# A 128-row lead-in with in-place LayerNorm, and crossbar DMA transposes for blocks 1 to 3, in a fused attention and GEGLU kernel

## The chip, the cores and the metric

The kernel runs on one core of a Trainium2 chip. Its time is device microseconds of one execution; the median of several executions is compared. The engines are TensorE (PE for matmuls, PEld for its weight loads), VectorE (DVE), ScalarE (ACT), GpSimd (POOL) and SyncE (SP), which issues every DMA of this kernel. Each engine runs its own instruction list in order and waits on semaphores.

## The reference

The input x is 2048 rows of 512. It is normalized, and the result xn goes through two branches whose outputs are added to x.

```python
xn = (x - mean(x)) / sqrt(var(x) + 1e-5)              # per row
# branch A: 32 heads of 16, sliding window of 8 positions, 2 apart
q, k, v = split(xn @ wqkv)                             # wqkv [512, 1536]
logits[s, w] = q[s] . k[s - 2*w] / 4                   # masked where s - 2*w < 0
o[s] = sum_w softmax(logits)[s, w] * v[s - 2*w]
A = o @ wo                                             # [512, 512]
# branch B
B = (gelu_tanh(xn @ w_gate) * (xn @ w_up)) @ w_down    # 512 -> 1376 -> 512
out = x + A + B
```

All inputs, weights and the output are bf16.

## The kernel before, in words

**Blocks and stages.** The rows are worked in 4 blocks of 512 (`b`), each of two pairs `p` of 128-row tiles `t`. One block goes through these stages, with the names of their tiles:

1. LayerNorm: x comes from memory into XIN, two tiles at a time (L906 for pair 0, L910 for the others). DVE makes the statistics `st` (L921) and their aggregate `mv` (L925); POOL adds epsilon, `ve` (L930 for block 0, L948 for the others), and raises it to the power 0.5, `sq` (L936, L954); DVE takes the reciprocal, `rstd` (L942, L960). DVE subtracts the mean from XIN into a second buffer XN (L968) and scales it there (L975). XIN and XN have 2 slots of two tiles each.
2. Transpose: TensorE transposes the 128x128 pieces of XN through an identity into PSUM (L991), and ACT evicts them to `xnT` (L1002), which has the model dimension on the partitions. In block 0 that is done tile by tile (4 transposes), in the other blocks by pairs (8).
3. Projections: TensorE multiplies `Wqkv` with `xnT` (L1046) in groups of four matmuls, one for each 128 rows of the contraction. ACT evicts to QT (L1069), KT (L1076) and VT (L1083); VT goes to a scratch in memory (L1090). Block 0 is cut into two halves of 256 rows (`NHALF` is [2, 1, 1, 1]), so its matmuls are 256 columns wide; in the others they have 512.
4. Attention: DVE multiplies QT with shifted views of KT, eight products PROD of 128x2048 (L1105); TensorE sums them over the head dimension (L1120) into logits; softmax runs on DVE and ACT (L1153 to L1183), and the probabilities go through memory to the layout PT (L1191, L1198). Shifted bands BS of V come from memory (L1209), DVE multiplies them with PT (L1224, "PV products"), TensorE sums (L1243), and ACT evicts to OT (L1254).
5. Feed-forward: for each of 11 hidden tiles `j` (the last has 96 rows) two groups of four matmuls, with Wg and Wu (L1274); ACT applies GELU into GG (L1284) and evicts UU (L1291), and DVE multiplies them into HT (L1296).
6. Output: for each 128-row tile one PSUM sum of 11 matmuls with Wd (L1321) and four with Wo (L1334). DVE adds the row XR of x, loaded again (L1306), into OB (L1364), which is stored (L1371). The last two tiles are done in two halves.

Before the first transpose TensorE runs 9 warm-up matmuls on zeros (L855), two more behind the first transposes and four behind the second; all of them come before the first projection.

**What sets the order.** The program is a graph of tasks. Each task names its engine, an estimated duration, the items it reads and writes, and a priority. Buffers are slots of pools, and PSUM is a pool of 8 banks with a quota for each use. At build time a planner (`schedule`) places the tasks one by one on a modelled clock, by priority among those that can start early enough, and the result is a fixed instruction list for each engine. `order_after` adds an order between two tasks that share no data. The planner is run several times, and the pass with the shortest modelled time is taken. A DMA in the model takes a fixed time and a transfer time, and the transfers follow one another. So each edit to tasks, pools or priorities can change the order of everything behind it.

The lines that choose a block's order of work:

```python
base = b * PB_ + (p % 2) * 10 - 30 - (LN_SHIFT if b > 0 else 0)   # LayerNorm, LN_SHIFT = 960
base = b * PB_ - CHAIN_SHIFT[b]                                   # projections, attention, output
fb = FFN_BASE + b * FFN_STEP                                      # feed-forward: 500 + 1000 b
sched = dict(PE_SLACK=1.6, DMA_BPUS=250e3, ...)
```

A lower number goes first, so LayerNorm of a block is placed nearly a block ahead of its projections, and feed-forward of a block fills TensorE beside the attention of the same and the next block.

Of the kernel before, what the change touches and what calls it, by code (L numbers as in the profile page):

```python
# [141 lines left out]
class Graph:  # L142
# [118 lines left out]
    def schedule(self, params=None, prior=None):  # L261
# [86 lines left out]
        while nsched < ntot:  # L348
# [6 lines left out]
            for t in ready:  # L355
# [305 lines left out]
def bass_parallel_sum__sliding_local_dilated__glu_gated_geglu__prompt_kernel(nc, A_x, A_wqkv, A_wo, B_x, B_w_gate, B_w_up, B_w_down, out, dbg=None, cfg=None):  # L661
    cfg = dict(cfg or {})
    NXIN = cfg.get("NXIN", 2)
    NXN = cfg.get("NXN", 2)
    NQT = cfg.get("NQT", 2)
    NXT = cfg.get("NXT", 3)
    NPROD = cfg.get("NPROD", 4)
    NMS = cfg.get("NMS", 2)
    ACC_SPLIT = cfg.get("ACC_SPLIT", False)
    FIN_PE_FROM = cfg.get("FIN_PE_FROM", 99)  # L670
    FIN_PE = cfg.get("FIN_PE", False)
# [13 lines left out]
                                    acc=(4 if ACC_SPLIT else 2)))  # L685
# [5 lines left out]
    NHALF = cfg.get("NHALF", [2, 1, 1, 1])  # L691
    PVR_MERGE = cfg.get("PVR_MERGE", 2)
    R_ACCD = cfg.get("R_ACCD", 400)
# [11 lines left out]
    with contextlib.ExitStack() as es:  # L705
# [19 lines left out]
        mhalf = sb("mhalf", [128, 2], F32)  # L725
# [4 lines left out]
        mv = sb("mv", [128, NT, 2], BF)  # L730
        ve = sb("ve", [128, NT], F32)
        sq = sb("sq", [128, NT], BF)
# [3 lines left out]
        XN = sb("XN", [128, NXN, 2, 512], BF)  # L736
# [26 lines left out]
        P_xn = Pool("xn", NXN)  # L763
# [29 lines left out]
        I_mhalf = Item("mhalf")  # L793
# [4 lines left out]
        I_mv = Item("mv")  # L798
        I_ve = Item("ve")
        I_rstd = Item("rstd")  # L800
# [48 lines left out]
        WARM = cfg.get("WARM", (9, 2, 4))  # L849
# [10 lines left out]

        for i, nm in enumerate(("q", "k", "v")):
# [4 lines left out]
            G.task("sp", "ld_w" + nm, 0, mk(), wr=[(I_wq, nm)], prio=-900 + i, nbytes=512 * 1024)  # L866
# [3 lines left out]
        for ci, nj in enumerate(WCH):  # L870
# [4 lines left out]
            for (nm, Wx, I_w, src) in (("g", Wg, I_wg, B_w_gate), ("u", Wu, I_wu, B_w_up)):  # L875
                def mk(Wx=Wx, src=src, c_lo=c_lo, c_hi=c_hi):
                    return lambda e: e.dma_start(
                        Wx[:, :, c_lo:c_hi], src[:, c_lo:c_hi].rearrange("(k p) n -> p k n", p=128))
                G.task("sp", "ld_w%s%d" % (nm, ci), 0, mk(), wr=[(I_w, ci)], prio=R_WG + 2 * ci + (nm == "u"),
                       nbytes=(c_hi - c_lo) * 1024)  # L880
            j0 += nj
        G.task("sp", "ld_wd0", 0, lambda e: e.dma_start(
            Wd[:, 0:10, :], B_w_down[0:1280, :].rearrange("(j p) n -> p j n", p=128)),
            wr=[(I_wd, 0)], prio=R_WD, nbytes=1280 * 1024)
        G.task("sp", "ld_wd1", 0, lambda e: e.dma_start(
            Wd[0:96, 10, :], B_w_down[1280:1376, :]), wr=[(I_wd, 1)], prio=R_WD + 1, nbytes=96 * 1024)
        for d4 in range(4):
# [4 lines left out]
            G.task("sp", "ld_wo%d" % d4, 0, mk(), wr=[(I_wo, d4)], prio=R_WD + 2 + d4, nbytes=128 * 1024)  # L892
# [4 lines left out]
        for p in range(NP):  # L897
# [10 lines left out]
            else:  # L908
# [3 lines left out]
                G.task("sp", "ld_x%d" % p, 0, mk_ld(), wr=[(it_x, 0), (it_x, 1)], prio=-950 + p * 20,  # L912
# [4 lines left out]
            for t2 in range(2):  # L917
# [4 lines left out]
                G.task("dve", "bnst%d" % t, d_dve(512, 1.2), mk_st(), rd=[(it_x, t2)], wr=[(I_st, t)], prio=tp0(t))  # L922
# [3 lines left out]
                G.task("dve", "bnag%d" % t, 0.15, mk_ag(), rd=[(I_st, t)], wr=[(I_mv, t)], prio=tp0(t) + 1)  # L926
            if b == 0:
                for t in (2 * p, 2 * p + 1):
                    def mk_ve(t=t):
                        return lambda e: e.tensor_scalar(  # L930
                            out=ve[:, t:t + 1], in0=mv[:, t, 1:2], scalar1=1e-5, scalar2=1.0,
                            op0=ALU.add, op1=ALU.mult)
                    G.task("pool", "ve%d" % t, 0.19, mk_ve(), rd=[(I_mv, t)], wr=[(I_ve, t)], prio=tp0(t) + 2)

                    def mk_sq(t=t):
                        return lambda e: e.tensor_tensor(  # L936
                            out=sq[:, t:t + 1], in0=ve[:, t:t + 1], in1=mhalf[:, 0:1], op=ALU.pow)
                    G.task("pool", "sq%d" % t, 0.7, mk_sq(), rd=[(I_ve, t), I_mhalf], wr=[(I_sq, t)],
                           prio=tp0(t) + 3)

                    def mk_rs(t=t):
                        return lambda e: e.reciprocal(out=rstd[:, t:t + 1], in_=sq[:, t:t + 1])  # L942
                    G.task("dve", "rstd%d" % t, 0.15, mk_rs(), rd=[(I_sq, t)], wr=[(I_rstd, t)], prio=tp0(t) + 3)
            else:
                tt = (2 * p, 2 * p + 1)

                def mk_ve(p=p):
                    return lambda e: e.tensor_scalar(  # L948
                        out=ve[:, 2 * p:2 * p + 2], in0=mv[:, 2 * p:2 * p + 2, 1], scalar1=1e-5, scalar2=1.0,
                        op0=ALU.add, op1=ALU.mult)  # L950
                G.task("pool", "ve%d" % p, 0.19, mk_ve(), rd=[(I_mv, t) for t in tt], wr=[(I_ve, p)], prio=base + 2)

                def mk_sq(p=p):
                    return lambda e: e.tensor_tensor(  # L954
                        out=sq[:, 2 * p:2 * p + 2], in0=ve[:, 2 * p:2 * p + 2], in1=mhalf[:, :], op=ALU.pow)
                G.task("pool", "sq%d" % p, 0.75, mk_sq(), rd=[(I_ve, p), I_mhalf], wr=[(I_sq, t) for t in tt],
                       prio=base + 3)

                def mk_rs(p=p):
                    return lambda e: e.reciprocal(out=rstd[:, 2 * p:2 * p + 2], in_=sq[:, 2 * p:2 * p + 2])  # L960
# [480 lines left out]
```

## Time and profile before

| | |
|---|---|
| median of 3 executions | 207.98 us (207.72 to 208.19) |
| profiled execution | 207.99 us |
| span from its first to its last instruction | 206.2 us |
| granted TensorE clock | 1.000 |
| TensorE matmuls busy | 197.7 us, 96% of the span |
| DVE busy | 148.7 us, 72% |
| ACT busy | 109.9 us, 53% |
| POOL busy | 13.5 us, 7% |

Busy time is the union of an engine's instructions. An instruction row has its start, its duration, the engine, the line, the operation and the tiles; several like ones are merged (x8), and their duration is then that of the stretch. In brackets stands how long the engine was idle before, and what it waited for. Matmuls overlap: a 512-column matmul has a duration of 379 ns, but one starts about every 0.216 us. The chain of work goes back from the last instruction to what released each step. PEld is the weight load, which may run beside the matmul before it.

### The profile page before, as it was taken

Reading aid. Unit: us, or ns where it says so; the run is one execution under the profiler, and the core shown is the slowest. Engines: PE = TensorE matmul, PEld = TensorE weight load, DVE = VectorE, ACT = ScalarE, POOL = GpSimd, SP = SyncE. Lnnn points to the kernel's source line nnn. Section 1 sums busy time; section 2 is a strip of 40 time slices with the busy share of each in tenths; the row PEclk is TensorE's granted clock in tenths of the full one; section 3 lists DMA queues with packets and bytes.
Section 4 is the critical chain, followed back from the end, with each engine's and each line's share of the span. In section 5 each row is a group of like instructions: output and inputs, shape, how many; then the busy total and the mean of one; then the engine's idle time right before and its main releaser. Section 6 shows DMA issues by size and latency. Waiting matters only on the chain.

```text
span 206.2 us, 3162 instructions
## 1 busy us (share of the span) xinstructions
PE 197.7 (96%) x1197; PEld 93.4 (45%) x1197; DVE 148.7 (72%) x221; ACT 109.9 (53%) x188; POOL 13.5 (7%) x42
## 2 busy tenths in 40 slices
PE   7799999999899999999999999999999999997993
PEld 2487353444434445444443444433444443443483
DVE  3728799988999958968999949799775846122121
ACT  2476556996772007679849005784995005765000
POOL 6610011022000110000000000000000000000000
PEclk9999999999999999999999999999999999999999
DMA  5999936843548331044870173567021522000121
GB/s 163 378 400 356 225 93 166 212 96 114 137 131 205 97 102 54 7 107 132 206 163 0 55 201 104 133 146 184 0 51 52 156 78 76 0 3 0 40 74 38
DMA packets 27070, 25.45 MB, mean 123 GB/s; under 512 B 2896, under 2 KB 25520, under 8 KB 27056
## 3 DMA queue, kind: packets, MB, share of 16 engines
q1 hardware_dynamic: 27056, 25.26, 44.6%
q8 instruction: 9, 0.15, 0.3%
q14 instruction: 5, 0.04, 0.1%
HBM read 19.99 MB, written 5.26 MB: 122 GB/s over the span
## 4 chain that ended last, share of the span: by engine, by line
PE 66%; DVE 21%; DMA 5%; issue 3%; POOL 2%; ACT 1%; SPq 0%; DVEq 0%
PE PS L1274 22%; PE PS L1321 19%; PE PS L1046 12%; DVE PVS L1224 8%; PE PS L1334 7%; DVE PROD L1105 4%; DMA PT<-pt_scratch 3%; PE PS L1243 2%; PE PS L1120 2%; DVE HT L1296 2%; DVE st L921 2%; DMA pt_scratch<-PB 1%; DMA XIN<-in_A_x_dram 1%; DVE XN L975 1%; PE PS L991 1%
## 5 line engine op out<-in xcount | busy, mean ns | idle before, releaser
L1274 PE MATMUL PS<-xnT,Wu 128*128 128x512 bf16 (+1 forms) x176 | 45.3, 380 | 0.0
L1274 PE MATMUL PS<-xnT,Wg 128*128 128x512 bf16 (+1 forms) x176 | 45.2, 379 | 0.0
L1046 PE MATMUL PS<-xnT,Wqkv 128*128 128x512 bf16 (+1 forms) x240 | 43.7, 337 | 0.3 <-ACT xnT L1002 0.3
L1321 PE MATMUL PS<-Wd,HT 128*128 128x512 bf16 (+3 forms) x198 | 41.0, 356 | 1.3 <-DVE HT L1296 1.1
L1224 DVE TENSOR_TENSOR PVS<-BS,PT 128x2048 bf16<-128x2048 bf16 x32 | 37.2, 1219 | 6.8 <-DMA PT<-pt_scratch 5.1
L1105 DVE TENSOR_TENSOR PROD<-QT,KT 128x2048 bf16<-128x2048 bf16 x32 | 37.2, 1218 | 6.3 <-ACT KT L1076 5.0
L1046 PEld LDWEIGHTS PS<-xnT,Wqkv 128*128 128x128 bf16 x240 | 22.9, 98 | 19.9 <-ACT xnT L1002 1.1
L1291 ACT ACTIVATE UU<-PS 128x512 bf16<-128x512 f32 (+1 forms) x44 | 26.7, 607 | 9.3 <-PE PS L1274 9.0
L1284 ACT ACTIVATE GG<-PS 128x512 bf16<-128x512 f32 (+1 forms) x44 | 26.8, 609 | 7.4 <-PE PS L1274 5.1
L1321 PEld LDWEIGHTS PS<-Wd,HT 128*128 128x128 bf16 (+1 forms) x198 | 19.1, 98 | 20.8 <-DVE HT L1296 2.2
L1296 DVE TENSOR_TENSOR HT<-GG,UU 128x512 bf16<-128x512 bf16 (+1 forms) x44 | 17.3, 419 | 13.6 <-ACT UU L1291 13.5
L1274 PEld LDWEIGHTS PS<-xnT,Wu 128*128 128x128 bf16 (+1 forms) x176 | 16.8, 100 | 21.7 <-issue 2.5
L1274 PEld LDWEIGHTS PS<-xnT,Wg 128*128 128x128 bf16 (+1 forms) x176 | 17.0, 100 | 20.7 <-issue 0.8
L1364 DVE TENSOR_TENSOR OB<-PS,XR 128x512 bf16<-128x512 f32 (+1 forms) x18 | 11.3, 627 | 18.9 <-PE PS L1334 18.8
L1002 ACT ACTIVATE xnT<-PS 128x1024 bf16<-128x1024 bf16 (+1 forms) x10 | 8.5, 852 | 22.5 <-PE PS L991 22.5
L1076 ACT ACTIVATE KT<-PS 128x512 bf16<-128x512 f32 (+1 forms) x20 | 10.1, 515 | 14.4 <-PE PS L1046 14.3
L1254 ACT ACTIVATE OT<-PS 128x512 bf16<-128x512 f32 x16 | 8.7, 594 | 16.1 <-PE PS L1243 16.0
L1334 PE MATMUL PS<-Wo,OT 128*128 128x512 bf16 (+1 forms) x72 | 16.8, 354 | 0.0
L1083 ACT ACTIVATE VT<-PS 128x512 bf16<-128x512 f32 (+1 forms) x20 | 10.2, 513 | 5.7 <-PE PS L1046 5.6
L921 DVE BATCH_NORM_STATS2 st<-XIN 128x6 f32<-128x512 bf16 x16 | 10.5, 683 | 3.0 <-DMA XIN<-in_A_x_dram 3.0
L1069 ACT ACTIVATE QT<-PS 128x512 bf16<-128x512 f32 (+1 forms) x20 | 10.2, 512 | 2.9 <-PE PS L1046 2.6
L1334 PEld LDWEIGHTS PS<-Wo,OT 128*128 128x128 bf16 x72 | 7.0, 97 | 6.9
(50 smaller groups left out, 110.5 us busy)
## 6 DMA issues: line engine op xcount, KB each, us to landing
BS<-vt_scratch SPq DMA_DIRECT2D x64, 128.5 KB, 3.5
XR<-in_A_x_dram SPq DMA_DIRECT2D x16, 128.0 KB, 2.4
XIN<-in_A_x_dram SPq DMA_DIRECT2D x7, 256.0 KB, 7.8
out_dram<-OB SPq DMA_DIRECT2D x14, 128.0 KB, 1.7
Wqkv<-in_A_wqkv_dram SPq DMA_DIRECT2D x3, 512.0 KB
vt_scratch<-VT SPq DMA_DIRECT2D x12, 128.0 KB
Wg<-in_B_w_gate_dram SPq DMA_DIRECT2D x1, 1376.0 KB
Wu<-in_B_w_up_dram SPq DMA_DIRECT2D x1, 1376.0 KB
```

What stands on the lines that cost most here:

```text
L921: return lambda e: e.bn_stats(out=st[:, t, :], in_=XIN[:, it.slot, t2, :])
L1046: ins = e.matmul(PS[:, 512 * it.slot:512 * it.slot + HWD], lhsT=lhsT, rhs=xnT[:, itx.slot, kt, c0:c0 + HWD], start=(kt == 0), stop=(kt == 3))
L1069: return lambda e: e.activation(out=QT[:, ito.slot, g, o:o + HWD], in_=PS[:, 512 * it.slot:512 * it.slot + HWD], func=ACTF.Identity)
L1105: return lambda e: e.tensor_tensor(out=PROD[:, it.slot, :, :], in0=bass.AP(QT, (itq.slot * 4 + g) * 512, [[NQT * 4 * 512, 128], [0, 4], [1 ...
L1224: return lambda e: e.tensor_tensor(out=bass.AP(PVS, (ito.slot * 2 + half) * 2048, [[NPVS * 4096, 128], [512, 4], [128, 4], [1, 128]]), in0 ...
L1274: ins = e.matmul(PS[0:M, 512 * it.slot:512 * it.slot + 512], lhsT=Wx[:, kt, j * 128:j * 128 + M], rhs=xnT[:, itx.slot, kt, :], start=(kt = ...
L1284: return lambda e: e.activation(out=GG[0:M, ito.slot, :], in_=PS[0:M, 512 * it.slot:512 * it.slot + 512], func=ACTF.Gelu_apprx_tanh)
L1291: return lambda e: e.activation(out=UU[0:M, ito.slot, :], in_=PS[0:M, 512 * it.slot:512 * it.slot + 512], func=ACTF.Identity)
L1296: return lambda e: e.tensor_tensor(out=HT[0:M, ito.slot, j, :], in0=GG[0:M, ig.slot, :], in1=UU[0:M, iu.slot, :], op=ALU.mult)
L1321: ins = e.matmul(PS[:, 512 * it.slot:512 * it.slot + CW], lhsT=HT[0:K, ith.slot, j, ti * 128:(ti + 1) * 128], rhs=Wd[0:K, j, c0:c1], start ...
L1334: ins = e.matmul(PS[:, 512 * it.slot:512 * it.slot + CW], lhsT=OT[:, ito.slot, dq, ti * 128:(ti + 1) * 128], rhs=Wo[:, dq, c0:c1], start=F ...
L1364: return lambda e: e.tensor_tensor(out=OB[:, ito.slot, 0:CW], in0=PS[:, 512 * it.slot:512 * it.slot + CW], in1=XR[:, itx.slot, c0:c1], op= ...
```

## The change

LayerNorm is done in place: XN is gone, XIN has 4 slots, and subtraction and scaling write XIN. The epsilon add goes from POOL to DVE; the first tile's subtraction goes to ACT, with its sign turned, which the scaling turns back. Block 0's LayerNorm gets a hand-written order on DVE. Block 0's Q and K are projected tile by tile, 16 matmuls of 128 columns in one PSUM bank for each of Q and K, with one eviction; its V is done in one piece with 512 columns. The first projection needs only the first tile. One warm-up matmul instead of six stands behind the first transposes.

In blocks 1 to 3 a DMA issued by SP transposes each normalized tile from XIN straight into `xnT`; their TensorE transposes and evictions are gone. The loads are reordered: Wq before the second pair of x, pairs 2 and 3 ahead of Wg; Wg and Wu wait for Wk to land; Wd and Wo follow in a fixed order; the XR rows of a block are loaded after its sixth GELU.

The output sum of a block's first tile is cut in two tasks: 4 matmuls with Wo and 8 with Wd, which need hidden tiles 0 to 7 alone, and then the last 3. The first waits by order for the block's last feed-forward group. In the planner, a task that follows another on its own engine by order alone is ready at that one's end; for DMAs that is the end of the issue, where it was the landing. Options that were off (`ACC_SPLIT`, `FIN_PE`) are removed.

```diff
@@ schedule
-                    rdy = max(rdy, p.done + lat)
+                    if p.eng == t.eng and p in t.odeps:
+                        rdy = max(rdy, p.end)
+                    else:
+                        rdy = max(rdy, p.done + lat)
@@ parameters and buffers
-    NXIN = cfg.get("NXIN", 2)
-    NXN = cfg.get("NXN", 2)
+    NXIN = cfg.get("NXIN", 4)
+    NSUBA = cfg.get("NSUBA", 1)
+    JA = cfg.get("JA", 8)
-    NHALF = cfg.get("NHALF", [2, 1, 1, 1])
+    NHALF = cfg.get("NHALF", [1, 1, 1, 1])
-        XN = sb("XN", [128, NXN, 2, 512], BF)
-        WARM = cfg.get("WARM", (9, 2, 4))
+        WARM = cfg.get("WARM", (9, 1))
@@ loads
+                t_w.deps.add(t_ld["wk"])
+        G.order_after(t_w, t_ld["u"])
-                G.task("sp", "ld_x%d" % p, ..., prio=-950 + p * 20,
+                G.task("sp", "ld_x%d" % p, ..., prio=(0, -899.5, -897.5, -897)[p] if p < 4 else -950 + p * 20,
...
+                G.order_after(t_xr, t_of["gelu%d_5" % b])
@@ LayerNorm
+                t_of["ve%d" % t] = G.task("dve", "ve%d" % t, 0.15, mk_ve(), ...)
+                if t < NSUBA:
+                    def mk_sub(t=t, t2=t2, it=it_x):
+                        return lambda e: e.activation(
+                            out=XIN[:, it.slot, t2, :], in_=XIN[:, it.slot, t2, :], func=ACTF.Identity,
+                            scale=-1.0, bias=mv[:, t, 0:1])
...
+            if b > 0:
+                for t2 in range(2):
+                    def mk_tr(p=p, t2=t2, it=it_x, itx=XTI[b]):
+                        o = 256 * (p % 2) + 128 * t2
+                        return lambda e: e.dma_start_transpose(
+                            xnT[:, itx.slot, :, o:o + 128], XIN[:, it.slot, t2, :])
+                    G.task("sp", "trx%d_%d" % (p, t2), 0, mk_tr(), rd=[(it_x, t2)],
+                           wr=[(XTI[b], (p % 2, t2))], prio=base + 4, nbytes=128 * 1024)
+                continue
...
+        chain(["bnst0", "bnag0", "ve0", "bnst1", "rstd0", "norm0", "bnag1", "ve1", "sub1", "bnst2", "rstd1",
+               "norm1", "bnag2", "ve2", "sub2", "bnst3", "rstd2", "norm2", "bnag3", "ve3", "sub3", "rstd3",
+               "norm3"])
@@ projections of block 0
+                                for g in range(4):
+                                    for kt in range(4):
+                                        ins = e.matmul(
+                                            PS[:, 512 * it.slot + 128 * g:512 * it.slot + 128 * g + 128],
+                                            lhsT=Wqkv[:, kt, which * 512 + g * 128:which * 512 + (g + 1) * 128],
+                                            rhs=xnT[:, itx.slot, kt, t * 128:(t + 1) * 128],
+                                            start=(kt == 0), stop=(kt == 3))
...
+                chain(warm_tasks[:WARM[0]] + ["tpx0_0"] + warm_tasks[WARM[0]:] +
+                      ["mmt0_0", "tpx0_1", "mmt1_0", "mmt0_1", "tpx1_0", "mmt1_1", "tpx1_1",
+                       "mmt0_2", "mmt1_2", "mmt0_3", "mmt1_3"])
@@ output
+                    if ti == 0:
+                        ja, jb = list(range(JA)), list(range(JA, NJ))
+                        t_a = G.task("pe", "acca" + sfx, d_mm(CW, 4 + len(ja)), mk_acc(ja, True, False),
+                               rd=[(it_ht, j) for j in ja] + [I_wd, it_ot, I_wo], wr=[it_acc],
+                               prio=base + 60, **acc_kw)
+                        G.order_after(t_a, t_of["fu%d_10" % b])
+                        G.task("pe", "accb" + sfx, d_mm(CW, len(jb)), mk_acc(jb, False, True),
+                               rd=[(it_ht, j) for j in jb] + [I_wd, it_acc], wr=[it_acc],
+                               prio=base + 59.5, **acc_kw)
```

More of the change, by code (lines that the diff above doesn't have):

```diff
@@ L927, in bass_parallel_sum__sliding_local_dilated__glu_gated_geglu__prompt_kernel @@
[L927 to L947, printed above, removed]
+                t_of["bnag%d" % t] = G.task("dve", "bnag%d" % t, 0.15, mk_ag(), rd=[(I_st, t)], wr=[(I_mv, t)], prio=tp0(t) + 1)
@@ L956, in bass_parallel_sum__sliding_local_dilated__glu_gated_geglu__prompt_kernel @@
[L956 to L960, printed above, removed]
[L961 to L963 removed]
+                        out=sq[:, t:t + n], in0=ve[:, t:t + n], in1=mhalf[:, 0:n], op=ALU.pow)
@@ L981, in bass_parallel_sum__sliding_local_dilated__glu_gated_geglu__prompt_kernel @@
+            for grp in ((0,), (1,)):
                 n = len(grp)
```

214 lines of the change are left out of this document (102 added, 112 removed).

## The prediction, made before the result was known

> **What bounds the kernel now.** I read first the page's busy shares, then TensorE's waits between 20 and 190 us, then busy time by stretch, then the chain of work that ended last, then the order of time in the first 20 us.
>
> ```profile
> span 206.2 us, 3162 instructions
> PE 197.7 (96%) x1197; PEld 93.4 (45%) x1197; DVE 148.7 (72%) x221; ACT 109.9 (53%) x188; POOL 13.5 (7%) x42
> GB/s 163 378 400 356 225 93 166 212 96 114 137 131 205 97 102 54 7 107 132 206 163 0 55 201 104 133 146 184 0 51 52 156 78 76 0 3 0 40 74 38
> 8.51:20.30 11.79, 11.79 (x106) 9.78 (x106) 5.91 (x10) 8.20 (x23) 1.90 (x7) 1.00 1.06 381
> 20.30:203.20 182.90, 180.07 (x1072) 81.50 (x1069) 137.44 (x197) 99.00 (x162) 6.12 (x12) 1.00 0.40 103
> 36.08:63.80 27.72, 26.47 (x161) 11.66 (x161) 26.39 (x42) 22.29 (x37) 2.36 (x4) 1.00 0.53 138
> PE PS L1243 <- DVE PVS L1224: 1.2, 2, 0.8
> PE PS L1321 <- DVE HT L1296: 1.1, 1, 1.1
> ```
>
> In the stretch rows the columns are length, then busy time of PE, PEld, DVE, ACT, POOL, granted clock, DMA share and GB/s. From 20.30 to 203.20 us TensorE is busy 180.07 of 182.90 us at clock 1.00, so only 2.83 us can come from removing waits there; 2.3 us are the two named waits (columns: total, times, longest). The other engines have long idle stretches, though DVE is at 26.39 of 27.72 us between 36 and 64. TensorE is the bound: what shortens the kernel is an earlier start of its useful stream, matmuls taken out of it, or one of those waits. The profiled execution took 207.99 us, 1.79 more than its span and 0.01 above the median of 207.98; sums below are on 207.99.
>
> **Term 1: the lead-in.** Columns: start, duration, engine, line.
>
> ```profile
> 0.80 2.18 DMA XIN<-in_A_x_dram
> 3.00 0.69 DVE L921 BATCH_NORM_STATS2 st<-XIN 128x6 f32<-128x512 bf16 x1 [3.00 <-DMA XIN<-in_A_x_dram]
> 3.73 0.18 DVE L925 BATCH_NORM_AGGREGATE mv<-st 128x2 bf16<-128x6 f32 x1
> 3.94 0.35 DVE L968 TENSOR_SCALAR XN<-XIN,mv 128x512 bf16<-128x512 bf16 x1
> 4.00 0.35 POOL L930 TENSOR_SCALAR ve<-mv 128x1 f32<-128x1 bf16 x1 [1.05 <-DVE mv L925]
> 4.43 0.57 POOL L936 TENSOR_TENSOR sq<-ve,mhalf 128x1 bf16<-128x1 f32 x1
> 5.04 0.16 DVE L942 RECIPROCAL rstd<-sq 128x1 f32<-128x1 bf16 x1
> 5.24 0.35 DVE L975 TENSOR_SCALAR XN<-XN,rstd 128x512 bf16<-128x512 bf16 x1
> 5.65 0.40 PE L991 MATMUL PS<-ident,XN 128*128 128x128 bf16 x4 [0.40 <-DVE XN L975]
> 6.08 0.60 ACT L1002 ACTIVATE xnT<-PS 128x512 bf16<-128x512 bf16 x1 [3.80 <-PE PS L991]
> 8.51 1.91 PE L1046 MATMUL PS<-xnT,Wqkv 128*128 128x256 bf16 x16
> 8.67 1.75 PE PS L1046 x16
> 10.42 0.22 PE PS L991 x4
> 20.45 0.86 PE PS L1274 x4
> ```
>
> Before, the first projection waits for two 128-row tiles and starts at 8.51. A 256-column matmul costs 1.75/16 = 109 ns, four transposes 0.22. Without the feed-forward groups that are interleaved, block 0's 96 projection matmuls and the last two transpose groups end at 8.51 + 96 x 0.109 + 0.44 = 19.4.
>
> After, the stream starts behind one tile. In order on DVE: statistics to 3.69, aggregate to 3.91; the epsilon add, now DVE, takes about 0.16 (as the 128x1 reciprocal) against POOL's 0.35 and two engine crossings; POOL's power 4.2 to 4.8, under which the second tile's statistics run; the first subtraction runs on ACT, 0.60 as a 128x512 eviction, to about 4.6. Reciprocal 4.87, scaling ends 5.41, transposes 5.45 to 5.85, eviction to 6.48, first Q matmul 6.5. The in-place scaling removes no instruction; it saves only buffers.
>
> Each later tile costs DVE 0.69 + 0.18 + 0.16 + 0.35 + 0.16 + 0.35 = 1.9 plus some 0.07 of gaps, so tiles are normalized at 5.4, 7.4, 9.35, 10.95. A tile gives TensorE 32 matmuls of 128 columns and 4 transposes. No Q or K matmul here has 128 columns yet; the nearest rows are these transposes, each with its own weight load:
>
> ```profile
> 34.35 0.61 PE L991 MATMUL PS<-ident,XN 128*128 128x128 bf16 x8
> 34.80 1.03 PE L1274 MATMUL PS<-xnT,Wg 128*128 128x512 bf16 x4
> 35.00 1.02 ACT L1002 ACTIVATE xnT<-PS 128x1024 bf16<-128x1024 bf16 x1 [1.57 <-PE PS L991]
> 36.08 1.04 PE L1046 MATMUL PS<-xnT,Wqkv 128*128 128x512 bf16 x4 [0.25 <-ACT xnT L1002]
> L1046 PEld LDWEIGHTS PS<-xnT,Wqkv 128*128 128x128 bf16 x240 | 22.9, 98 | 19.9 <-ACT xnT L1002 1.1 <-issue 0.8 <-ACT OT L1254 0.4
> ```
>
> Eight take 0.45 before the next group starts: 56 ns each. The other bound is the whole weight load, 98 ns, if loads ceased to overlap. I take 56: same width, same number of loads. Q and K then cost 128 x 56 = 7.2 (7.0 before), V 16 x 216 = 3.5 (a group of 4 with 512 columns takes 0.865, L1274), three later transpose groups 0.66: 11.3 from 6.5, so 17.8 without waits. I add 0.5 for waits on tiles 2 to 4 and on ACT, which has three 0.6 us jobs per 2.0 us tile (between 0 and 1.6): 18.3, against 19.4. **Gain 1.1** (0 to 1.6). Five warm-up matmuls fewer lie inside this.
>
> The weights must keep up. SP now issues x tiles 0 and 1, Wq, the next rows, Wk, Wv, all remaining prefetched rows, then waits for Wk's landing before Wg and Wu. From the GB/s line (5.155 us a slice: 0.84 MB by 5.2, 2.79 MB by 10.3): Wq is complete after 0.79 MB, at 5 us, before 6.5; Wk after 1.57 MB at 7.1, wanted near 7.7: the tightest. Behind the wait stand only Wg, Wu, the pad store, Wd and Wo. 2.6 MB are queued when it ends, busy until 9.9, and a load's first data needs about 2.2 from issue (x, 0.80 to 2.97), so the transfers have no hole; Wg (1.41 MB) lands near 13.4, Wu near 17, before V ends. Cost zero; if Wk came 1 us late, the gain of term 1 would vanish.
>
> **Term 2: the transposes of blocks 1 to 3.** Six groups of 8 leave TensorE, each displacing what follows by 0.45: **2.7**, and the 0.25 wait at 36.08 goes with the eviction: **0.2**. Six 1.02 us evictions leave ACT; at 53% busy that is worth nothing. Twelve DMAs of 128 KB come in, on SP's queue. Their issue is priced by a load, 0.38 each (first row below), 4.6 us of SP in all, spread over three blocks. Behind a transpose that waits at SP's head for DVE's scaling stand the band loads BS and the PT reload, for which DVE's PV products wait; the XIN loads stand in that queue now in the same way, and the PV waits of TensorE come to 1.2 us in all with them. What hides their latency:
>
> ```profile
> 27.37 0.38 SPq L910 DMA_DIRECT2D XIN<-in_A_x_dram  x1
> XR<-in_A_x_dram SPq DMA_DIRECT2D x16, 128.0 KB, 2.4
> Wo<-in_A_wo_dram SPq DMA_DIRECT2D x4, 128.0 KB, 9.0
> 32.62 0.62 DVE L975 TENSOR_SCALAR XN<-XN,rstd 128x512 bf16<-128x512 bf16 x2
> 80.70 0.61 DVE L968 TENSOR_SCALAR XN<-XIN,mv 128x512 bf16<-128x512 bf16 x2
> 103.37 0.61 PE L991 MATMUL PS<-ident,XN 128*128 128x128 bf16 x8
> ```
>
> A DMA transpose is not in this trace. Same-size transfers land in 2.4 us, or 9.0 behind the weights. Block 1's last rows were normalized at 33.24 and block 1's first projection ran at 36.08, so there is no cover in the old order; but block 0's feed-forward, 22 groups of 4 matmuls at 0.865 = 19.0 us, can run from 18.3 to 37.3 in its place, and the rows now come in before 10 us, so DVE can normalize them earlier (it was idle 5.9 of the 11.8 us from 8.5 to 20.3). Block 3's rows were normalized near 81 and transposed at 103. So 2.4 is hidden everywhere, 9.0 costs 33.24 + 9.0 - 37.3 = 4.9 once, and only if DVE keeps its old order. I take 2.4 to 4: zero.
>
> [...]
>
> **Term 3: the output sum, split for the first tile of a block.** The last lines of the chain:
>
> ```profile
> 175.60 0.98 PE PS L1243 x16
> ...
> 184.89 3.90 PE PS L1274 x18
> 188.81 0.60 ACT UU L1291
> 189.43 0.43 DVE HT L1296
> 189.91 2.55 PE PS L1321 x11
> ```
>
> At 188.8 TensorE ends the last feed-forward group and waits for hidden tile 10. Now 4 Wo matmuls and 8 Wd matmuls (tiles 0 to 7; tile 10 is made at 189.9 and a tile takes 8 x 0.216 = 1.73, so tile 7 at 184.7) come first: 12 x 0.216 = 2.6 us, more than the 1.14 wait. **Gain 1.1.** The cover is OT, whose last sums (L1243) end at 176.6; were OT later than 188.8, the wait would stay. The row XR loads now wait for a GELU; XR is read only when an output tile ends, so zero. Behind the last matmul, 3.0 us of the span, nothing changes.
>
> **Others.** The epsilon adds put 10 x 0.16 = 1.6 on DVE, the first subtraction takes 0.35 off; DVE has 28% idle, but where it is at 95% (36 to 64) this may lengthen the two PV waits (0.8 and 0.4 us) by 0.3. Against that, block 0's eight products can run from about 15.6 in one stream and end near 25; the last now ends at 31.1:
>
> ```profile
> 29.96 1.12 DVE PROD L1105
> ```
>
> I put 0.4 of the 1.2 down as saved, bounds -1.2 (the waits double) and +1.2 (they go). The planner reorders everything: no row prices that.
>
> Sum: 1.1 + 2.7 + 0.2 + 1.1 + 0.4 = 5.5; 207.99 - 5.5 = **202.5**.
>
> **Rivals.**
> Waits take the place of the removed work: DVE's chain (products, softmax, PV) sets the first output sum or a projection, as it does in the chain between 22 and 60 us. For it: 95% DVE there. Against: TensorE still found filler and idled 1.25 of 27.7 us. Giving half back: 205.2.
> 128-column matmuls run at their weight load, 98 ns: 128 x 42 ns = 5.4, so 207.9, no change. Against it the 56 ns of L991. [...]
> Slower: the transposes land late at one place, block 1's first projection. With DVE's old order the stall is 33.24 + L - 37.3 for a landing time L; it eats the gain from L = 9.6 us and shows as slower from 10.1; at L = 12, 7.9 of stall give 210.4. [...] Against: the nearest unloaded row, 2.4, and the earlier rows.
> The lead-in gains nothing (Wk late, or DVE slower per tile): 203.6.
>
> **How the numbers follow.** Forecast 202.5 with its own range 200.9 to 203.5: 0.63. Lead-in without gain: 0.06. Waits in exchange: 0.17. Weight-load pace: 0.05, half of it faster, half no change. Transposes late: 0.09, of which 0.01 is no change. 200.9 is the floor of the terms: 207.99 less 1.6, 2.7 and all 2.83 us of idle. The range 200.6 to 206.2 reaches a little under it, because short waits may hide in the modelled ends of matmuls, and over the exchange of waits; it leaves out about 0.15. A difference within 0.2% (0.42 us) is about what cannot be told from none: faster 0.88, same 0.04, slower 0.08.
>
> **What would show it.** Right: first Q matmul near 6.5 and Q, K at 56 ns; no L991-type groups after 12 us; a first output matmul of block 3 within 0.1 us of the last feed-forward one; TensorE idle below 3 us between 20 and the last matmul. Wrong: a wait of TensorE on a DMA into xnT at a block's first projection; transposes that take far over 4 us; new DVE waits at L1243 or the output sums; Q and K matmuls at 80 to 98 ns.

## The result, and the profile after

The changed kernel takes 201.71 us (median of 4, 201.42 to 201.96) against 208.08 for the kernel before beside it: ratio 0.9696, 95% interval 0.9676 to 0.9715. The profiled execution took 201.42 us, 6.57 less than the profiled one before; its span is 6.5 shorter.

The head, the busy shares and the chain's shares by engine, from the page after:

```profile
span 199.7 us, 3150 instructions
PE 194.4 (97%) x1192; PEld 89.5 (45%) x1192; DVE 149.2 (75%) x230; ACT 104.7 (52%) x171; POOL 10.4 (5%) x32
PE 93%; DMA 2%; ACT 2%; DVE 1%; SPq 1%; issue 0%; DVEq 0%
```

TensorE was the bound and is more so: 3.3 us less work, 97% busy. The lead-in after, from the rows in order of time (TensorE, then one of DVE):

```profile
6.60 1.07 PE L1045 MATMUL PS<-xnT,Wqkv 128*128 128x128 bf16 x16 [0.47 <-ACT xnT L1008]
7.87 0.40 PE L997 MATMUL PS<-ident,XIN 128*128 128x128 bf16 x4 [0.21 <-DVE XIN L972]
8.20 1.96 PE L1045 MATMUL PS<-xnT,Wqkv 128*128 128x128 bf16 x32
6.67 0.69 DVE L925 BATCH_NORM_STATS2 st<-XIN 128x6 f32<-128x512 bf16 x1 [0.75 <-DMA XIN<-in_A_x_dram]
```

and the end of block 0's projections in the chain (start, length):

```profile
11.50 3.57 PE PS L1045 x64
15.07 3.45 PE PS L1089 x16
```

The first Q matmul runs at 6.60 where 8.51 stood before. 64 matmuls of 128 columns in 3.57 us are 55.8 ns each. V ends at 18.52; by the chain of before (8.67 + 96 x 0.109 + 0.44) it was 19.6. Of the 1.9 us of earlier start, 0.8 does not arrive there, most of it in holes; the largest lies between the first tile's Q, which ends at 7.67, and its K at 8.20, and only 0.22 of it is the transposes between them. They wait for the second tile, which is scaled at 7.81: the third tile's statistics stand ahead of it on DVE and wait 0.75 for x.

The stretch from there to the last matmul, and TensorE's only wait in it:

```profile
18.36:197.08 178.72, 178.13 (x1023) 78.59 (x1021) 135.66 (x191) 94.08 (x153) 3.58 (x5) 1.00 0.51 118
```

```profile
PE PS L1274 <- ACT UU L1322: 0.5, 1, 0.5
```

The change-over from feed-forward to output at the end, and block 0's products, in order of time:

```profile
182.97 1.03 PE L1305 MATMUL PS<-xnT,Wu 128*96 128x512 bf16 x4
183.83 1.03 PE L1351 MATMUL PS<-Wo,OT 128*128 128x512 bf16 x4
15.74 9.17 DVE L1135 TENSOR_TENSOR PROD<-QT,KT 128x2048 bf16<-128x2048 bf16 x8 [0.25 <-ACT KT L1064]
```

In this stretch TensorE is idle for 0.59 us, against 2.83 before. The 1.14 us ahead of the first output sum is gone (183.83 follows 182.97 at the pace of four matmuls), so are both waits on PV products, and one of 0.5 has come. The DMA transposes as a group (min, median and max of an issue in ns; then the time from the start of an issue to its landing, where the trace has it; it has none for block 1's first pair):

```profile
L981 SPq DMA_TRANSPOSE xnT<-XIN x12: 1195/1209/2412, 20.9 to 102.4; - x12
DMA to landing us min/median/max: 2.4/2.9/3.9
```

Block 1's transposes and block 0's V stores on SP's queue, and block 1's first projection:

```profile
20.91 4.49 SPq L981 DMA_TRANSPOSE xnT<-XIN  x2
25.45 4.75 SPq L1120 DMA_DIRECT2D vt_scratch<-VT  x4
30.24 2.51 SPq L981 DMA_TRANSPOSE xnT<-XIN  x2
36.51 1.03 PE L1089 MATMUL PS<-xnT,Wqkv 128*128 128x512 bf16 x4
```

The last transpose of block 1 is issued at 31.5 and lands 3.1 us later, near 34.6, 1.9 ahead of the projection, which waits for nothing. What holds the pair back to 30.24 is SP's queue: its rows are ready at 26.86 (the row below, of DVE), and the four V stores stand ahead of it.

```profile
26.25 0.61 DVE L972 TENSOR_SCALAR XIN<-XIN,rstd 128x512 bf16<-128x512 bf16 x2
```

**The account.** Lead-in 1.1; transposes off TensorE 2.7; idle in the long stretch 2.83 - 0.59 = 2.2; the tail behind the last matmul 0.4 (199.7 - 197.06 = 2.6, against 206.2 - 203.15 = 3.05). Sum 6.4 of 6.5. The ends of the last matmuls, before and after, from the two chains:

```profile
202.70 0.45 PE PS L1334 x4
195.84 1.22 PE PS L1356 x11
```

The last store is issued 0.9 us behind the last matmul in both kernels, so the 0.4 lies behind that issue. That it belongs to the change is not shown (see the last term below).

### The profile page after: what moved, and what is told of

Read it like the earlier page. It is cut to its first block, busy times and chain, and to the rows that moved or that the text cites. A ratio compares the mean times of both kernels' runs of the same rounds, so it can differ in the third digit from the quotient of the medians.

```text
span 199.7 us, 3150 instructions
## 1 busy us (share of the span) xinstructions
PE 194.4 (97%) x1192; PEld 89.5 (45%) x1192; DVE 149.2 (75%) x230; ACT 104.7 (52%) x171; POOL 10.4 (5%) x32
## 4 chain that ended last, share of the span: by engine, by line
PE 93%; DMA 2%; ACT 2%; DVE 1%; SPq 1%; issue 0%; DVEq 0%
PE PS L1305 37%; PE PS L1356 19%; PE PS L1089 17%; PE PS L1351 7%; PE PS L1151 4%; PE PS L1274 4%; PE PS L1045 3%; DMA XIN<-in_A_x_dram 2%; ACT L1315 1%; ACT OT L1285 1%; ACT UU L1322 0%; PE PS L997 0%; SPq L910 0%; DVE st L925 0%; ACT GG L1315 0%
## 5 line engine op out<-in xcount | busy, mean ns | idle before, releaser
L1089 PE MATMUL PS<-xnT,Wqkv 128*128 128x512 bf16 x160 | 35.9, 379 | 0.0
L1305 PEld LDWEIGHTS PS<-xnT,Wu 128*128 128x128 bf16 (+1 forms) x176 | 16.6, 100 | 22.9 <-issue 3.4
L1376 DVE TENSOR_TENSOR OB<-PS,XR 128x512 bf16<-128x512 f32 (+1 forms) x18 | 11.3, 628 | 19.7 <-PE PS L1356 18.5
L1089 PEld LDWEIGHTS PS<-xnT,Wqkv 128*128 128x128 bf16 x160 | 15.4, 98 | 19.0 <-issue 0.4
L1106 ACT ACTIVATE KT<-PS 128x512 bf16<-128x512 f32 x12 | 7.2, 597 | 13.3 <-PE PS L1089 13.3
L1099 ACT ACTIVATE QT<-PS 128x512 bf16<-128x512 f32 x12 | 7.2, 596 | 12.8 <-PE PS L1089 12.6
L1113 ACT ACTIVATE VT<-PS 128x512 bf16<-128x512 f32 x16 | 9.6, 598 | 4.7 <-PE PS L1089 4.7
L942 POOL TENSOR_TENSOR sq<-ve,mhalf 128x2 bf16<-128x2 f32 (+1 forms) x10 | 6.7, 666 | 68.5 <-DVE ve L936 68.5
## 6 DMA issues: line engine op xcount, KB each, us to landing
BS<-vt_scratch SPq DMA_DIRECT2D x64, 128.5 KB, 3.1
```

The costliest lines, as they stand in the source:

```text
L1089: ins = e.matmul(PS[:, 512 * it.slot:512 * it.slot + HWD], lhsT=lhsT, rhs=xnT[:, itx.slot, kt, c0:c0 + HWD], start=(kt == 0), stop=(kt == 3))
L1305: ins = e.matmul(PS[0:M, 512 * it.slot:512 * it.slot + 512], lhsT=Wx[:, kt, j * 128:j * 128 + M], rhs=xnT[:, itx.slot, kt, :], start=(kt = ...
L1376: return lambda e: e.tensor_tensor(out=OB[:, ito.slot, 0:CW], in0=PS[:, 512 * it.slot:512 * it.slot + CW], in1=XR[:, itx.slot, c0:c1], op= ...
```

## The experiments

Theory S: three gains that add up (an earlier stream, TensorE transposes removed, waits removed), and the DMA transposes are hidden because the rows reach DVE early. Its rivals were that the transposes only exchange one wait for another, and that the lead-in or the split bring nothing.

### One part undone

**a_tensor_tr**: the changed kernel with TensorE transposes and evictions again in blocks 1 to 3.

```diff
-            if b > 0:
...
-                        return lambda e: e.dma_start_transpose(
...
-            for grp in ((0,), (1,)):
+            for grp in ((0,), (1,)) if b == 0 else ((0, 1),):
```

> The changed kernel, but blocks 1 to 3 transpose on TensorE again, by pairs, with ACT evictions. Theory W (TensorE's work sets the time): six groups of 8 matmuls come back at 0.45 us each, so +2.7 us against 201.7, 204.4. Rival P (the gain came from the planner's new order and fewer waits): within 0.5 us of 201.7, or an amount that has nothing to do with 2.7.

204.45 us (204.22 to 204.8), 2.7 more than the changed kernel. No wait appears behind the lead-in. One of its six transpose groups:

```profile
43.17 0.61 PE L988 MATMUL PS<-ident,XIN 128*128 128x128 bf16 x8
```

Six times 0.45 is 2.7: the groups come back at the price forecast, and they exchange no wait. That the times differ by just as much is partly luck. In the profiled executions V ends 0.6 later here (x landed later at the start) and the tail is 0.4 longer, while the 0.6 of idle in the long stretch is gone.

**a_one_sum**: the changed kernel with the first output sum in one task.

```diff
-                    if ti == 0:
+                    if False:
```

> The changed kernel with the output sum of a block's first tile in one task again (Wo matmuls first, as now). Theory W: only block 3 has nothing else to run behind its last feed-forward group, so the old wait of 1.1 us for hidden tile 10 returns there and nowhere else: 202.8. Rival P: the planner hides it, 201.7.

202.30 us (202.02 to 202.39), 0.6 more, where 1.1 was expected. The wait comes back where and as long as expected:

```profile
184.42 1.04 PE L1351 MATMUL PS<-Wo,OT 128*128 128x512 bf16 x4 [1.14 <-DVE HT L1327]
```

But the planner's new order has lost the 0.5 at L1274, which pays half of it back. The mechanism holds; the net is less than the wait.

**a_two_tiles**: the first projection behind the second tile's transposes.

```diff
-                       ["mmt0_0", "tpx0_1", "mmt1_0", ...
+                       ["tpx0_1", "mmt0_0", "mmt1_0", ...
```

> The changed kernel, but the first projection waits for the second tile's transposes, as before. Theory W: the first projection starts near 8.9 instead of 6.6 us and Q, K and V then run without a hole (7.2 + 0.44 + 3.5), so they end near 20.0 instead of 18.5: +1.5, 203.2. Rival: the lead-in is off the path, because DVE's chain of block 0 sets what follows: 201.7.

204.18 us, from 202.96 to 205.11. In the profiled execution (202.96):

```profile
7.83 0.40 PE L997 MATMUL PS<-ident,XIN 128*128 128x128 bf16 x4 [1.62 <-DVE XIN L972]
8.06 2.84 PE L1045 MATMUL PS<-xnT,Wqkv 128*128 128x128 bf16 x48
15.66 3.62 PE L1089 MATMUL PS<-xnT,Wqkv 128*128 128x512 bf16 x16
```

The stream starts at 8.06, earlier than the expected 8.9, and V ends 0.74 later than in the changed kernel, with x landing at the same time: starting behind one tile is worth that much. The rest of the spread goes with the granted clock: 202.96 and 203.46 at 0.998, 204.91 and 205.11 at 0.991 and 0.992.

### One part alone

**b_split**: the kernel before with the split output sum only (and, as in the changed kernel, the Wo matmuls ahead of those with Wd in every output sum).

```diff
+                    if ti == 0:
+                        ja, jb = list(range(JA)), list(range(JA, NJ))
...
+                        G.order_after(t_a, t_of["fu%d_10" % b])
```

> The kernel before, with only the split of a block's first output sum. Theory W: the 1.1 us wait behind block 3's last feed-forward group goes and nothing else moves: 206.9. Rival P (the planner's new order decides): an amount between 206 and 209 that does not match.

206.29 us (206.08 to 206.57), ratio 0.9907, 0.9875 to 0.9939: 1.7 less, where 1.1 was expected. TensorE from 20.30 to its last matmul:

```profile
20.30:201.60 181.30, 179.90 (x1073) 81.90 (x1071) 137.50 (x197) 99.41 (x162) 6.12 (x12) 1.00 0.41 104
```

Idle is 1.4 us against 2.83: the 1.1 of the wait, 0.2 from the PV waits, and 0.1 in small ones.

**b_xbar**: the kernel before with the DMA transposes only, from XN.

```diff
+            if b > 0:
+                for t2 in range(2):
+                    def mk_tr(p=p, t2=t2, ito=it_xn, itx=XTI[b]):
+                        ...
+                            xnT[:, itx.slot, :, o:o + 128], XN[:, ito.slot, t2, :])
...
```

> The kernel before, with only one thing of the change: blocks 1 to 3 transpose by crossbar DMA, out of XN, whose two slots stay. Theory W (TensorE's work sets the time, the DMA is hidden): the six groups go, 2.7 us and the 0.25 us wait, 205.1. Rival D: without the early loads and the four slots the transposed rows of block 1 come late (2.9 us to landing after 1.2 us of issue, against 1.7 us by TensorE and ACT), and 1 us or more is given back: 206 or above.

208.45 us (10 executions), ratio 1.0036, 1.0004 to 1.0068: no gain at all, as rival D had it (206 or above). TensorE's wait, then the scaling of the second pair's rows on DVE and their issue on SP, then two stretches behind the wait:

```profile
PE PS L1055 <- DMA xnT<-XN: 3.5, 1, 3.5
```

```profile
31.16 0.62 DVE L975 TENSOR_SCALAR XN<-XN,rstd 128x512 bf16<-128x512 bf16 x2
33.88 2.52 SPq L984 DMA_TRANSPOSE xnT<-XN  x2
```

```profile
38.00:40.00 2.00, 2.00 (x6) 0.73 (x5) 1.93 (x3) 0.14 (x1) 0.00 (x0) 0.50 0.53 127
42.00:44.00 2.00, 2.00 (x11) 0.92 (x10) 1.12 (x4) 0.81 (x2) 0.00 (x0) 1.00 1.09 223
```

The second pair of block 1 is issued at 33.88 and lands at 37.64, past the end of the feed-forward work that could cover it. Its rows are ready at 31.78, 4.9 later than in the changed kernel; the other 2.1 to the issue go to V stores and a load of x ahead of it on SP's queue. After the wait TensorE runs at a granted clock of 0.50 until 40.8. So the part that is worth 2.7 us in the whole change is worth nothing by itself. What else of the change hides it was the open question, and the next runs answer it.

**b_inplace4**: b_xbar, with the rows normalized in place in four XIN slots (the memory of two XIN and two XN slots), and pairs 2 and 3 of x loaded behind Wv.

```diff
-    NXIN = cfg.get("NXIN", 2)
+    NXIN = cfg.get("NXIN", 4)
-        XN = sb("XN", [128, NXN, 2, 512], BF)
+        XN = XIN
-            it_xn = Item("xn%d" % p, P_xn, "x")
+            it_xn = it_x
-                G.task("sp", "ld_x%d" % p, ..., prio=-950 + p * 20,
+                G.task("sp", "ld_x%d" % p, ..., prio=(-950, -930, -897.5, -897)[p] if p < 4 else -950 + p * 20,
```

> The kernel before, with the crossbar transposes for blocks 1 to 3, the normalized rows written in place into four XIN slots (two XIN and two XN slots before, the same memory), and the second and third further pairs of x loaded behind Wv. No new lead-in, no split sum, no new planner rule. Theory E (what hides the DMA transposes is that the rows come early enough to be normalized ahead of block 0's products): DVE normalizes block 1's rows before or beside its eight products, the last transposes are issued by 31 and land by 34, no wait of TensorE on xnT at block 1's first projection (3.5 us in the kernel with the transposes alone), and the 2.7 us of the removed TensorE transposes appear: 208.0 - 2.7 = 205.3, between 204.6 and 206.0. Rival D (the DMA path is too slow or too much in the way, whatever the buffers): a wait of 2 us or more on xnT stays, and the time is 207.5 or more.

203.50 us (203.35 to 203.72), ratio 0.9781, 0.9767 to 0.9796: 4.65 less than before, 4.95 less than b_xbar. Its head, TensorE's one long wait behind the lead-in, and the second pair of block 1:

```profile
span 201.7 us, 3064 instructions
```

```profile
PE PS L1330 <- DVE HT L1305: 1.4, 1, 1.4
```

```profile
29.26 3.08 SPq L984 DMA_TRANSPOSE xnT<-XIN  x2
```

The pair is issued 4.6 us sooner and the wait on xnT is gone. Its rows are ready at 26.55, since block 1's LayerNorm, all but the last scaling, now lies ahead of block 0's products on DVE. The 1.2 us of waits on PV products are gone too. 2.7 + 0.25 + 1.2, a tail 0.4 shorter and the wait on HT 0.3 longer make 4.25 of the 4.5 in the spans. The expectation (205.3) had left the PV waits and the tail out.

**a_xin2**: the counterpart, the changed kernel with two XIN slots.

```diff
-    NXIN = cfg.get("NXIN", 4)
+    NXIN = cfg.get("NXIN", 2)
```

> The kernel after with two XIN slots instead of four (NXIN = 2), so that block 1's rows are loaded only when block 0's are transposed. Theory E: block 1's rows are normalized behind block 0's eight products (past 25), its last transposes are issued past 30 and land past 33, and TensorE waits on xnT at block 1's first projection for 1 to 4 us, with slow matmuls behind the wait as in the kernel before with the transposes alone: 203.0 to 206.5. Rival H (a DMA transpose is hidden with either number of slots, since feed-forward groups of block 0 fill TensorE until 36): 201.7, within 0.5.

206.85 us (205.13 to 207.11), 5.1 more than the changed kernel and a little above the expected range. From the profiled execution, the one of 205.13:

```profile
PE PS L1089 <- DMA xnT<-XIN: 2.8, 1, 2.8
```

```profile
33.45 2.50 SPq L981 DMA_TRANSPOSE xnT<-XIN  x2
```

The wait of b_xbar is back, at the same place and with nearly the same issue time. Block 1's LayerNorm lies behind block 0's products, as expected, and the rows are ready at 32.54. In this execution the clock stayed up behind it (granted clock 0.999); in the four others it was 0.991 or 0.992, and they took 206.7 to 207.1.

### How much room the DMA transposes have

**a_tr_x2**, **a_tr_x4**: every DMA transpose issued two and four times.

```diff
+                    for rpt in range(2):      # 4 in a_tr_x4
-                        G.task("sp", "trx%d_%d" % (p, t2), 0, mk_tr(), rd=[(it_x, t2)],
+                        G.task("sp", "trx%d_%d_%d" % (p, t2, rpt), 0, mk_tr(), rd=[(it_x, t2)],
...
```

> The changed kernel with every DMA transpose issued twice, the second behind the landing of the first, so a tile lands after about 5.8 us instead of 2.9; the planner is told only of the second issue. Theory H (hidden: the rows are transposed well ahead): within 0.4 us of 201.7. Rival Q (SP's queue is held while the copies land, and band loads behind them come late): 202.5 to 204, with waits of DVE at the PV products.

207.72 us (206.11 to 209.07), 6 more. Neither expectation is right: the transposes aren't hidden, and the cost is not at the PV products. TensorE's wait:

```profile
PE PS L1090 <- DMA xnT<-XIN: 2.8, 1, 2.8
```

SP's queue ahead of it:

```profile
29.82 5.66 SPq L981 DMA_TRANSPOSE xnT<-XIN  x4
36.71 0.39 SPq L914 DMA_DIRECT2D XIN<-in_A_x_dram  x1
37.68 2.52 SPq L981 DMA_TRANSPOSE xnT<-XIN  x2
```

and the end of it in the chain:

```profile
34.21 2.48 DMA xnT<-XIN
38.94 2.50 DMA xnT<-XIN
41.52 1.87 PE PS L1090 x4
```

Four issues end at 35.5. Behind them stands a load of x into a slot that transposes still read: it is issued when the last of the four has landed (34.21 + 2.48 = 36.69), and the last two transposes stand behind it. They land at 41.44, and the first projection moves with them; its four matmuls then take 1.87 us instead of 0.86 (granted clock 0.51 from 41 to 43). So with twice the issues the landing moves by some 6.8 us, far more than the 2.5 us of issue added for a pair. Not all of the 6 us comes from this: in the profiled execution x and Wk landed later at the start, and block 0's projections ended 1.1 later than in the changed kernel.

> The same with four issues for each transpose: a tile lands after some 11.6 us, past the 9.6 us at which the prediction let the gain be used up at block 1's first projection. By the prediction's rival, a wait of TensorE at that projection, 207 to 210. Theory Q: SP is held some 140 us in all, and the first waits are those of DVE's PV products on BS and PT and of TensorE at L1274, not at the projections; 205 to 215. Theory H alone would give 201.7 to 202.5.

255.25 us in the profiled execution, far outside both ranges; a second one took 713.88, for which I have no cause. TensorE waits three times for xnT:

```profile
PE PS L1090 <- DMA xnT<-XIN: 41.9, 3, 21.6
```

```profile
31.11 14.94 SPq L981 DMA_TRANSPOSE xnT<-XIN  x8
```

An issue still takes 1.2 us (median of the run's 48: 1194 ns). The rest of the 14.94 is waiting between them, as a repeat waits for the copy before it to land (SP's queue waits 19.3 us for landings of transposes ahead of further ones, in 14 waits).

| kernel | last rows of block 1 ready | their transposes issued | TensorE waits on xnT |
|---|---|---|---|
| b_inplace4 | 26.55 | 29.26 | none |
| changed kernel | 26.86 | 30.24 | none |
| a_xin2 | 32.54 | 33.45 | 2.8 |
| b_xbar | 31.78 | 33.88 | 3.5 |
| a_tr_x2 | 28.02 | 37.68 (last two) | 2.8 |

Rows that are ready early come first; SP's queue then takes 0.9 to 3.4 us more, and in a_tr_x2 the added issues on that queue make the wait by themselves.

**a_old_rule**: the changed kernel with the planner's old rule for order alone.

```diff
-                    if p.eng == t.eng and p in t.odeps:
-                        rdy = max(rdy, p.end)
-                    else:
-                        rdy = max(rdy, p.done + lat)
+                    rdy = max(rdy, p.done + lat)
```

> The kernel after with the planner's old rule (a task that follows another on its engine by order alone waits for that one's full latency, for DMAs the landing). The planner then places Wd's and Wo's loads behind the first DMA transposes, and block 1's second pair of transposes behind three band loads BS on SP's queue. Theory S (SP's queue order decides when the transposes are issued, and a pair of transposes issued past 31 stalls block 1's first projection): the BS loads wait for the V stores, the second pair is issued past 31 and TensorE waits on xnT for 0.5 to 3 us with slow matmuls behind: 203 to 206. Rival P (the order of these loads is hidden, as the planner thinks): 201.7, within 0.6.

202.58 us (202.03 to 202.71), 0.9 more, outside the ranges of both. Theory S of this run fell: the second pair was issued at 28.74, ahead of the limit, and nothing waits on xnT. Most of the 0.9 is in short waits of another order:

```profile
PE PS L1271 <- ACT KT L1103: 0.7, 1, 0.7
PE PS L1271 <- DVE PVS L1252: 0.5, 1, 0.5
PE PS L1148 <- ACT OT L1282: 0.3, 1, 0.3
```

### The start

**a_stat_later**: on DVE, the third tile's statistics behind the second tile's scaling, since they wait 0.75 us for x.

```diff
-        chain([..., "sub1", "bnst2", "rstd1",
-               "norm1", "bnag2", ...
+        chain([..., "sub1", "rstd1",
+               "norm1", "bnst2", "bnag2", ...
```

> The changed kernel, in whose hand-written DVE order the third tile's statistics, which wait 0.75 us for x, stand behind the second tile's scaling instead of ahead of it. If that wait is what holds the second transposes to 7.87 us, they start near 7.5 and everything behind comes 0.3 to 0.4 us earlier: 201.3. Rival: the later statistics only move the hole to the third tile: 201.7.

201.27 us (200.8 to 202.19), 0.4 less than the changed kernel, with intervals that overlap. So whether it gains is not shown. The second transposes do move, from 7.87 to 7.54, but TensorE then waits for Wk, which landed some 0.6 later in this execution, and V ends at 19.1:

```profile
7.54 0.39 PE L997 MATMUL PS<-ident,XIN 128*128 128x128 bf16 x4
8.77 1.96 PE L1045 MATMUL PS<-xnT,Wqkv 128*128 128x128 bf16 x32 [0.84 <-DMA Wqkv<-in_A_wqkv_dram]
```

The landing of the first loads varies that much between executions: with the same loads in the same order, the third tile's statistics start at 6.61 in a_one_sum, at 6.67 in the changed kernel and at 7.84 in a_tr_x2. A start that differs by 0.5 us in one profile says little about an edit.

**a_lead2**: a_stat_later, and also the second pair of x as two tiles behind Wk, and the third tile's Q ahead of the fourth tile's transposes.

```diff
-            if p == 0:
+            if p < 2:
...
+                           prio=(-960, -898.8)[p] + 0.2 * t2, nbytes=128 * 1024)
...
-                       ["mmt0_0", "tpx0_1", "mmt1_0", "mmt0_1", "tpx1_0", "mmt1_1", "tpx1_1",
-                        "mmt0_2", "mmt1_2", "mmt0_3", "mmt1_3"])
+                       ["mmt0_0", "tpx0_1", "mmt1_0", "mmt0_1", "tpx1_0", "mmt1_1", "mmt0_2",
+                        "tpx1_1", "mmt1_2", "mmt0_3", "mmt1_3"])
```

> The kernel after with the start reordered: the second pair of x is loaded as two tiles behind Wk instead of as a pair ahead of it, the third tile's statistics follow the second tile's scaling on DVE, and TensorE does the third tile's Q projection ahead of the fourth tile's transposes. Theory L (the start is limited by which bytes come first: 0.5 MB take 1.5 us, and the pair of x stands ahead of Wk): Wk is complete near 7.4 instead of 8.15, the second transposes start near 7.5 instead of 7.87, the first K projection near 7.8 instead of 8.19, V ends near 18.1 instead of 18.53; 0.4 us less, 201.3 (200.9 to 201.5). Rival (the third and fourth tiles then come late by as much and the hole only moves to them): V ends at 18.5 or later and the time is 201.7 or more.

201.08 us (200.96 to 201.39), ratio 0.9667, 0.9652 to 0.9681: 0.6 less than the changed kernel and 0.2 less than a_stat_later, with intervals that overlap. If it is faster, it isn't for the reason expected. The hole has moved to the third tile, and V ends at about 19.1, later than 18.5:

```profile
8.11 0.69 DVE L927 BATCH_NORM_STATS2 st<-XIN 128x6 f32<-128x512 bf16 x1 [1.07 <-DMA XIN<-in_A_x_dram]
10.58 0.40 PE L999 MATMUL PS<-ident,XIN 128*128 128x128 bf16 x4 [0.44 <-DVE XIN L974]
15.72 3.40 PE L1091 MATMUL PS<-xnT,Wqkv 128*128 128x512 bf16 x15
```

The rival is right for the start: Wk came sooner (SP issued Wg behind it at 7.72 instead of 8.17) and the third tile's x later, so the other order only moved the wait. It is wrong for the time. What was gained lies behind the start: no wait at L1276 where the changed kernel has 0.5, and 0.3 more whose place is open.

## Why the prediction was right, point by point

**The bound** and **term 1** (1.1 predicted, 1.1 measured): first Q at 6.60 against 6.5, 55.8 ns against 56, V at 18.5 against 18.3. The rival at the weight load's pace is out: this trace gives 55.8 in a stream of load and matmul, where the loads still take 98 each beside the matmuls (from 11.50 to 15.07 PE is busy for 3.57 us and PEld for 3.51). The 80 ns at which the prediction let the sign of that rival begin is in no run, nor is a pace between 56 and 98 that would have made it "faster". The weak step was the loads. The second tile was normalized at 7.81 instead of 7.4, because x for the third tile came late, for which the prediction had no term. Wk, put at 7.1, landed near 8.15 (SP issued Wg behind it at 8.17). "If Wk came 1 us late, the gain would vanish" did not hold: it came 1 us late, and K, which the late second tile let start at 8.09 (7.87 + 0.22) at best, started at 8.20. The allowance of 0.5 for waits covered both. Of the 1.1, a_two_tiles shows 0.74 for the start behind one tile; the rest is not taken apart.

**Term 2** (2.7 + 0.2): 2.7 by the six groups of a_tensor_tr. One price in it was wrong by a factor of three: an issue takes 1.2 us of SP, not the 0.38 of a load, 16.6 us of SP in all instead of 4.6. It cost nothing because SP has the room at that moment, and a_tr_x2 shows how little room that is. The landing, put at 2.4 to 4, was 2.4 to 3.9 where the trace has it. The other price, 9.0 behind the weights, was real too: in a_tr_x2 block 1's first pair is issued at 21.34, behind the loads of Wo (issued until 20.65, 8.8 to landing), and the slowest of the run's transposes landed after 10.3, against a median of 3.2. That cost nothing, as the pair is issued 11 us or more ahead of its use (22.86 and 34.22 in b_inplace4, 20.91 and 36.51 in the changed kernel).

Away from the weights, the transposes land about as the other transfers of their size do: the median of 2.9 compares with 2.1 for the loads of XR (128 KB) and 3.1 for those of BS (128.5 KB). b_xbar's pair landed 3.8 us behind its first issue. Neither is near the 9.6 at which the slower rival has the gain eaten.

The cover was named rightly, block 0's feed-forward and rows that come early, and b_xbar, b_inplace4 and a_xin2 show that it is the second which decides. Of the in-place scaling the prediction said "it saves only buffers" and priced it at nothing. By instructions that is so; but those buffers are what lets the rows come early, and without them the whole of term 2 is gone. The slower rival had the right place, block 1's first projection, and too late a limit: the stall was to start at 33.24 + L = 37.3, so at L = 4; b_xbar stalls 3.5 us with landings of 2.5, since SP's queue and a first issue come before the second one's landing and the filler was used up at 34.2.

**Term 3** (1.1): the 1.14 us wait is gone in the changed kernel and in b_split, and back in a_one_sum.

**Others** (0.4, bounds -1.2 and +1.2): both PV waits went, 1.2, and 0.5 came: 0.7. The products of block 0 end at 24.9, as forecast (25). In b_xbar and b_inplace4 they also run in one stream, to 24.7 and 26.0, without the new lead-in, and the PV waits are gone there as well; b_split, whose last product still ends near 31, keeps 1.0 of them. That fits the reason given, but a_xin2 and a_old_rule end the products at 25.3 and wait 0.5 on PV, so it is not shown. **Not in the sum**: 0.4 at the tail, which the prediction held fixed at 3.0. It does not follow the transposes: with them b_xbar and b_inplace4 have 2.6 us behind the last matmul, but a_two_tiles 2.9 and a_tr_x2 3.1; without them b_split and a_tensor_tr have 3.05. Why stays open, and so whether the 0.4 belongs to the change. The 0.3 and the 0.4 make up most of what 202.5 was too high, 0.8 against the median and 1.1 against the profiled execution.

## What to carry to other kernels

A pair of transposes moved to DMAs saves its TensorE time only if the source is ready ahead of its consumer by one issue time, one landing and whatever stands ahead on the issuing queue (1.2 + 2.5 + 2.1 us in b_xbar); look first for the buffers that make the source early, and test the part alone, since it may be worth nothing without them. Price a DMA's issue from a row of its own kind (1.2 us for a transpose here, 0.38 for a load). When a planner orders the rest, expect each edit to move some half a microsecond of short waits either way.

## What the runs showed of the hardware

In two runs a wait of TensorE of about 3 us cost half as much again: in b_xbar TensorE is idle from 34.2 to 37.7, and the granted clock is 0.50 from 37.4 to 40.8; in the profiled execution of a_tr_x2 it is idle from 38.7 to 41.5, and the clock is 0.50 from 41.0 to 44.5. The ends of these stretches are estimates from the mean clocks of stretches of 2 us: 0.84, 0.50 and 0.80 from 36 to 42 in b_xbar, 0.51 and 0.63 from 41 to 45 in a_tr_x2. Both slow stretches are some 3.4 us long, and TensorE works for 3.1 and 3.0 us of them, which loses some 1.5 us. The ten executions of a_tr_x2 fall into steps: 206.1 at clock 0.997 and 1.000, 207.2 to 207.8 at 0.990 to 0.992, 208.9 to 209.1 at 0.984; 0.008 of 206 us is 1.6, or by estimate some 3.3 us at half clock, once or twice. What decides whether the clock falls is not shown: it fell 3.1 us into the wait of 3.5 in b_xbar and 2.4 us into that of 2.8 in a_tr_x2, but a_xin2's profiled execution kept its clock (1.00 from 33 to 43) through a wait of 2.8. The four others of a_xin2 have mean clocks of 0.991 and 0.992, but no trace.

A DMA transpose of 128x512 bf16 holds SP for 1.2 us (2.0 and 2.4 for the two issued among the weight loads), and lands 2.4 to 3.9 us behind the start of its issue in the changed kernel, and up to 10.3 in a_tr_x2, whose first pair is issued behind the loads of Wo.
